# Sparse attention feeding a squared-ReLU feed-forward: batch 0's global columns in two groups of head pairs, batch 1's first pair loaded between weight slices, and batch 1's masks on VectorE

## The chip, the cores and the metric

The kernel runs on one core of a Trainium2 chip. A core has five engines [...]: TensorE (PE in the profile; its weight loads are PEld), VectorE (DVE), ScalarE (ACT), GpSimd (POOL) and SyncE (SP). SP, POOL and ACT can also start DMA transfers[...]. The metric is the device time of one execution in microseconds. Of seven runs before the change the median is 328.26 us, the lowest 325.69 and the highest 331.1.

## The reference

Attention over 8 batches, 8 heads, 576 tokens and 64 numbers per head, with a window of 32 tokens to each side and 8 global tokens that see all and are seen by all; its output is the input of a feed-forward with a squared ReLU.

```
scores = (1/sqrt(D)) * q @ k.T                       # B=8, H=8, S=576, D=64
mask   = |i - j| <= 32  or  i global  or  j global   # 8 global tokens, given as indices
attn   = softmax(where(mask, scores, -1e9))
x      = (attn @ v), heads side by side: (4608, 512)
out    = relu(x @ w_in)**2 @ w_out                   # w_in (512, 2048), w_out (2048, 512)
```

## The kernel before, in words

Heads are worked on in pairs, four pairs to a batch; the text calls them pairs 0 to 31, so pairs 0 to 3 are batch 0 and pairs 4 to 7 batch 1. `NHP` is 4. A pair's scores are computed in two halves of query columns (`half` 0 and 1): `sc_mm` is the matmul, `sc_exp` the exponential on ACT, `sc_mask` a multiplication by a 0/1 mask on DVE, `pv_mm` the product with the values, `pv_rec` a reciprocal on ACT by logarithm and exponential, and `pv_mul` the division that puts the result into the transposed activations `xT` (or `xA`, a second buffer, for the first half of batch 0). Where `added(i, half)` is true, the mask isn't multiplied on DVE: two matmuls of an identity with the tile `far` put a large negative number into the score bank ahead of the scores.

The queries of the global tokens are computed as extra columns of each half. `pv_sum` adds their partial sums and, at the last pair of a group, divides them (`gr`, `gx`); `scatter` then copies the 8 global columns, one at a time, into place on POOL. The columns of batch 0 go into `xA` and, once more, into `xT`.

The feed-forward's work is cut into units. The first chunk of 512 tokens uses `mm1_half` (256 tokens, two blocks of hidden units; 8 matmuls) and `mm2`; the rest uses `mm1` and a fast form of the second product. Units stand in the list `fills`; `take(n)` places n of them, and `fill(n)` places about n, as far as the batches that they read are done. They keep TensorE busy between the dependent steps of attention. A unit's result goes through ACT (`rl`, the ReLU) and DVE (`gt`, the square).

The whole order of work on each engine is written out by hand. For batches 0 and 1 tokens are loaded with their rows across partitions (`fetch_tokens`, on POOL's queue, which also casts to 16 bits), cast or copied by DVE (`cast_tokens`, tiles `natk` and `natq`), transposed on TensorE (`transpose`) and put in place by DVE and ACT (`place_k`, `place_q`). Batch 1's values are loaded as fp32 by 20 transfers on SP's queue (`fetch_values`, line 161; five per pair) into `stv`, and cast pair by pair by DVE (`cast_values`, line 463). Ahead of these transfers SP issues a tiny transfer called `gate` (line 1012), which reads the last slice of `w_in` and so holds SP until that slice has landed. From batch 2 on POOL first copies k and q into DRAM in another order (`kscr`, `qscr`; lines 178 and 185), SP adds the rows of the global tokens (lines 446 and 193), and SP then issues DMA transposes that bring `kt` and `qt` straight into SBUF (lines 201 and 202).

The part that the change touches lies at lines 971 to 1060. Its order on POOL before: the four slices of `w_in` (line 973), k and q of pairs 4 to 6, the scatter of batch 0's pairs 0 to 2 and then of pair 3 into `xA`, k and q of pair 7, the four slices of `w_out` (line 1009), the scatter into `xT` (line 1010), and the gathers and copies for batch 2. On TensorE: the first four units of `mm1_half` without their last quarter of the contraction, the value products of pairs 2 and 3 (half 1), the last quarter of the four units, two more units, the transposes of pair 4, two more units, and then the loop over pairs 4 to 7 (line 1032). After the loop come `scatter(1)`, the first DMA transposes and `fill(3)`; then the loop over pairs 8 to 31 (line 1063).

[...]

Of the kernel before, what the change touches and what calls it, by code (L numbers as in the profile page):

```python
# [50 lines left out]
def kernel(  # L51
# [18 lines left out]
    NDM = dm // P  # L70
    NFF = dff // P
    NHP = H // 2
# [9 lines left out]
    def sbt(name, shape, dtype, bufs=1, tag=None):  # L82
        return sb.tile(shape, dtype, name=name, tag=(tag or name), bufs=bufs)
# [12 lines left out]
    def pst(tag, shape, dtype=FP32):  # L96
        return psum["pool"].tile(shape, dtype, name=tag, tag=tag, bufs=psum["bufs"][tag])
# [12 lines left out]
    def token_rows(nm, i):  # L110
        x = "kq".index(nm)
        if i < 2:
            one = stf[0:TP, x, 2 * FW * i : 2 * FW * (i + 1)]
        elif i < NHP:
            one = s16a[0:TP, x, 2 * FW * (i - 2) : 2 * FW * (i - 1)]
        else:
            one = s16b[0:TP, x, 2 * FW * (i - NHP) : 2 * FW * (i - NHP + 1)]
        return one.rearrange("p (h f) -> p h f", h=2)
# [22 lines left out]
    xA = mix[:, 8 * FW : 8 * FW + NDM * S].rearrange("p (t s) -> p t s", t=NDM)  # L141
# [8 lines left out]
    def fetch_tokens(eng, nm, i):  # L150
        b, hp = divmod(i, NHP)
        eng.dma_start(
            out=token_rows(nm, i),
            in_=src[nm][b, 2 * hp : 2 * hp + 2].rearrange("h (p j) d -> p h (j d)", j=TJ),
        )
# [140 lines left out]
    def halves(to, weights, moving, **flags):  # L296
        for r in column_tiles():
            nc.tensor.matmul(to[r], weights[:, r], moving, **flags)  # L298
# [143 lines left out]
    def gather_store(c, gsts, nms="kqv", eng=None):  # L442
        for nm in nms:
            gst = gsts[nm]
            scr = dram.tile([P, D], gst.dtype, name=f"gscr_{nm}{c}")
            (eng or nc.sync).dma_start(out=scr, in_=gst)
            gscr[(nm, c)] = scr.rearrange("(b g h) d -> b g h d", b=2, h=H)
# [5 lines left out]
    def cast_tokens(op, nm, i):  # L453
        nat = nats[(nm, i)] = sbt("nat" + nm, [TP, TJ, P], FP16, bufs=2)
        op(
            out=nat.rearrange("p j (h d) -> p h j d", d=D),
            in_=token_rows(nm, i).rearrange("p h (j d) -> p h j d", d=D),
        )
# [100 lines left out]
    def mm1_half(u, half, tiles=range(NDM)):  # L559

        if 0 not in gts:
            gts[0] = sbt("gt", [P, NFF, TC], FP16)
        if 0 in tiles:
            ph_now[u] = pst("mm", [P, 2, 256])
        ph = ph_now[u]
        for j in range(2):
            for t in tiles:
                halves(
                    ph[:, j], w_in[:, t, (u + j) * P : (u + j + 1) * P],
                    (xT if half else xA)[:, t, half * 256 : half * 256 + 256],  # L570
                    start=(t == 0 and j == 0), stop=(t == NDM - 1), skip_group_check=True,
                )
        if NDM - 1 not in tiles:
            return
        rl = sbt("rl", [P, TC], FP16, bufs=5).rearrange("p (j x) -> p j x", j=2)
        nc.scalar.activation(out=rl, in_=ph, func=AF.Relu)
        nc.vector.tensor_tensor(
            out=gts[0][:, u : u + 2, half * 256 : half * 256 + 256], in0=rl, in1=rl, op=ALU.mult
        )
# [145 lines left out]
    def take(n):  # L725
        for _ in range(n):
            _, fn, a = fills.pop(0)
            fn(*a)
# [5 lines left out]
    def fill(n):  # L734
        credit[0] += n
        while fills and fills[0][0] <= done[0]:
            cost = {mm1: W1, mm2_fast: W2}.get(fills[0][1], 1) * share[0]
            if credit[0] < cost / 2:
                break
            credit[0] -= cost  # L740
            take(1)
        else:
            credit[0] = min(credit[0], 0)
# [6 lines left out]
    scs, ets, accs, recs = {}, {}, {}, {}  # L750

    def added(i, half):
        return i < NHP and (half == 0 or i < 2) or NHP <= i < 2 * NHP and half == 0

    def sc_mm(i, half, idles=0):

# [43 lines left out]
    def pv_mm(i, half, idles=0):  # L800
        b, hp = divmod(i, NHP)
        et = ets.pop((i, half))
        acc = pst("at", [P, 2, 512])
        warm(acc[:, 0], idles)
        win, _ = windows(i, half)
        vt = vts[i] if b < 2 else vbs[b % 2][:, :, 2 * hp : 2 * hp + 2]
        for n, (t, so, c0, w) in enumerate(win):
            o = c0 - half * BANKC
            for x in range(2):
                for e in range(2):  # L810
                    nc.tensor.matmul(  # L811
                        acc[D * e : D * e + D, x, o : o + w], onesb if x else vt[:, t, e],
                        et[:, e, so : so + w],
                        start=(n == 0), stop=(n == len(win) - 1), skip_group_check=True,
                    )
        accs[(i, half)] = acc[:, :, 0:BANKC].rearrange("p x (k c) -> p x k c", c=GRP)

    def pv_rec(i, half):
        av = accs[(i, half)]
        rec = recs[(i, half)] = sbt("rec", [P, 2, GTOK], FP32, bufs=3)  # L820
        nc.scalar.activation(out=rec, in_=av[:, 1, :, 0:GTOK], func=AF.Ln)  # L821
        nc.scalar.activation(out=rec, in_=rec, func=AF.Exp, scale=-1.0)  # L822

    def pv_sum(i, half):
        b, hp = divmod(i, NHP)
        av = accs[(i, half)]
        if half == 0 or b:
            if hp == 0 and half == 0:
                gsum[b] = sbt("gs", [P, 2, NHP, 2, NG], FP32, bufs=2)
            nc.vector.tensor_reduce(  # L830
                out=gsum[b][:, half, hp],
                in_=av[:, :, :, GTOK:GRP].rearrange("p e k g -> p e g k"),
                axis=AX.X, op=ALU.add,
            )
        if (half == 0 and b == 0 and hp >= NHP - 2) or (half and b and hp == NHP - 1):
            gs = gsum[b][:, 0]
            a, z = (0, NHP) if b else (0, NHP - 1) if hp < NHP - 1 else (NHP - 1, NHP)
            if b:
                nc.vector.tensor_tensor(out=gs, in0=gs, in1=gsum[b][:, 1], op=ALU.add)
            gr = sbt("gr", [P, NHP, NG], FP32, bufs=2)  # L840
            if a == 0:
                gxs[b] = sbt("gx", [P, NHP, NG], FP16, bufs=2)
            nc.vector.reciprocal(out=gr[:, a:z], in_=gs[:, a:z, 1])
            nc.vector.tensor_tensor(
                out=gxs[b][:, a:z], in0=gs[:, a:z, 0], in1=gr[:, a:z], op=ALU.mult
            )

    def pv_mul(i, half):
        b, hp = divmod(i, NHP)
        av, rec = accs.pop((i, half)), recs.pop((i, half))  # L850
        x0 = b * S + half * HS
        nc.vector.tensor_tensor(  # L852
            out=(xT if x0 else xA)[:, hp, x0 : x0 + HS].rearrange("p (k x) -> p k x", k=2),
            in0=av[:, 0, :, 0:GTOK], in1=rec, op=ALU.mult,
        )

    def pv(i, half):
        pv_mm(i, half)
        pv_rec(i, half)
        pv_sum(i, half)  # L860
        pv_mul(i, half)
# [8 lines left out]
    def scatter(b, pairs=slice(0, NHP), x=xT):  # L870
        xb = x[:, pairs, b * S : (b + 1) * S]
        for g in range(NG):
            nc.gpsimd.tensor_copy(out=xb[:, :, ds(gv[g], 1)], in_=gxs[b][:, pairs, g : g + 1])  # L873
# [5 lines left out]
    pool = nc.gpsimd  # L879
# [90 lines left out]
    sc_mm(3, 1)  # L970
    gather_store(0, gs0, "v")
    for i in range(4):
        pool.dma_start(out=w_in[:, :, ts(i, 512)], in_=wv[:, :, ts(i, 512)])
    def tokens1(i):
        for nm in "kq":
            cast_tokens(vec, nm, i)

    def transposes1(i):
        transpose("k", i)
        transpose("q", i)  # L980
        place_k(i, act)
        place_q(i)

    for i in range(NHP, 2 * NHP - 1):
        fetch_tokens(pool, "k", i)
        fetch_tokens(pool, "q", i)
    scatter(0, slice(0, NHP - 1), xA)
    pv_rec(1, 1)
    sc_exp(2, 1)
    sc_exp(3, 1)  # L990
# [3 lines left out]
    open_psum(2, 4)  # L994
    wide[0] = True
    for u in range(0, 8, 2):
        mm1_half(u, 0, range(NDM - 1))
    pv(2, 1)
    pv(3, 1)
    scatter(0, slice(NHP - 1, NHP), xA)  # L1000
    fetch_tokens(pool, "k", 2 * NHP - 1)
    fetch_tokens(pool, "q", 2 * NHP - 1)
    nc.scalar.copy(out=xT[:, :, 256:HS], in_=xA[:, :, 256:HS])
    for u in range(0, 8, 2):
        fills.pop(0)
        mm1_half(u, 0, range(NDM - 1, NDM))
    tokens1(NHP)
    for j in range(4):
        pool.dma_start(out=w_out[:, ts(j, 4), :], in_=wo[:, ts(j, 4), :])
    scatter(0)  # L1010
# [9 lines left out]
    nc.gpsimd.memset(vbs[0][96:P, NT - 1], 0.0)  # L1020
    gather_store(1, gs1)
    take(2)
    transposes1(NHP)
    tokens1(NHP + 1)
    take(2)
    done[0] = 1
    for vt in vts[NHP:]:
        nc.vector.memset(vt[96:P, 4], 0.0)
# [28 lines left out]
    scatter(1)  # L1057
    fetch_transposed(2 * NHP)
    fetch_transposed(2 * NHP + 1)
    fill(3)  # L1060
    wide[0] = False

    for i in range(2 * NHP, B * NHP):
        b, hp = divmod(i, NHP)
# [66 lines left out]
```

## Time and profile before

| what | value |
|---|---|
| median of 7 runs | 328.26 us (325.69 to 331.1) |
| the profiled execution, its own time | 327.39 us |
| its span, first to last instruction | 325.7 us |
| TensorE busy | 311.1 us, 96% of the span, 4739 matmuls |
| VectorE busy | 244.6 us, 75% |
| ScalarE busy | 202.0 us, 62% |
| GpSimd busy | 127.9 us, 39% |
| packets moved by POOL's queue, by SP's queue | 16.78 MB, 21.23 MB |
| granted TensorE clock | 1.000 |

The profile is one execution. Its own time exceeds the span by 1.69 us, which lies before the first and after the last instruction. A busy share is a mean over stages that differ much, so the stage from 15 to 71 us, in which the edits lie, has to be read by itself: by the order of the instructions on each engine, by what ended each wait, and by what the two DMA queues moved.

### The profile page before, as it was taken

How to read it: one execution, taken by the hardware profiler on the slowest of the kernel's cores; microseconds unless marked ns; L12 is line 12 of the kernel's file. 1: busy time of each engine (PE TensorE's matmuls, PEld its weight loads, DVE VectorE, ACT ScalarE, POOL GpSimd, SP SyncE). 2: the span in 40 equal slices, each digit the busy share in tenths (PEclk: the TensorE clock that was granted, in tenths of full speed). 3: DMA queues.
4: the chain of work that ended last, by engine and by line, in shares of the span. 5: the costliest groups of instructions: out<-in, count | busy, mean ns of one | idle time of the engine just before them, and what ended most of it. 6: DMA issues, size and time to landing. Idle time of an engine off the chain costs nothing.

```text
span 325.7 us, 11457 instructions
## 1 busy us (share of the span) xinstructions
PE 311.1 (96%) x4739; PEld 235.8 (72%) x4739; DVE 244.6 (75%) x601; ACT 202.0 (62%) x380; POOL 127.9 (39%) x222
## 2 busy tenths in 40 slices
PE   7996899989999999999999999999999999999995
PEld 4665677445578758875899856985698569868995
DVE  6576598548997788677867869876987698768465
ACT  3567687535866686667557387658765876373150
POOL 8466985548701960189100980049302000100000
PEclk9999999999999999999999999999999999999999
DMA  8999999999993999499924599769996301200211
GB/s 187 177 179 203 196 196 158 161 122 206 145 102 60 177 177 117 77 175 145 143 71 109 48 170 153 74 110 189 134 104 125 102 0 34 97 3 2 83 50 66
DMA packets 149919, 39.32 MB, mean 121 GB/s; under 512 B 133124, under 2 KB 149300, under 8 KB 149868
## 3 DMA queue, kind: packets, MB, share of 16 engines
q0 software_dynamic: 95408, 16.78, 68.2%
q1 hardware_dynamic: 54042, 21.23, 34.6%
q8 instruction: 37, 0.61, 0.8%
q10 hardware_dynamic: 418, 0.59, 0.7%
q14 instruction: 14, 0.11, 0.1%
HBM read 37.86 MB, written 17.29 MB: 169 GB/s over the span
## 4 chain that ended last, share of the span: by engine, by line
issue 36%; PE 29%; POOL 10%; DMA 8%; DVE 4%; ACT 2%; POOLq 1%; SPq 0%; ACTq 0%
PE mm L298 25%; DMA qscr<-in_q_dram 3%; POOL xT L873 3%; POOL kscr L178 3%; DMA kscr<-in_k_dram 2%; DMA qt<-qscr 2%; PE at L811 2%; POOL s16b L207 1%; PE at L770 1%; DVE gt L545 1%; ACT er L779 1%; DVE mix L630 1%; POOL qscr L185 1%; PE mm L492 1%; DVE early L624 1%
## 5 line engine op out<-in xcount | busy, mean ns | idle before, releaser
L298 PE MATMUL mm<-xT,w_in 128*64 128x512 f16 (+2 forms) x1216 | 122.5, 351 | 0.2 <-POOL xT L873 0.2
L298 PEld LDWEIGHTS <-w_in 128*64 128x64 f16 (+1 forms) x1280 | 79.3, 109 | 44.8 <-issue 3.3
L543 ACT ACTIVATE rl<-mm 128x512 f16<-128x512 f32 x128 | 75.0, 598 | 36.1 <-PE mm L298 34.0
L298 PEld LDWEIGHTS <-mix 128*64 128x64 f16 x1280 | 68.8, 110 | 1.9 <-issue 0.3
L545 DVE TENSOR_TENSOR gt<-rl 128x512 f16<-128x512 f16 x128 | 52.9, 422 | 22.9 <-ACT rl L543 22.0
L873 POOL COPY xT<-gx 128x4 f16 x64 | 18.0, 282 | 129.3 <-DVE xT L852 125.7
L779 ACT ACTIVATE er<-at 128x880 f16<-128x880 f32 x54 | 46.1, 904 | 15.5 <-PE at L770 13.9
L630 DVE TENSOR_TENSOR mix<-gt 128x1024 f16<-128x1024 f16 (+1 forms) x82 | 52.8, 670 | 0.2
L789 DVE TENSOR_TENSOR et<-er,mask 128x880 f16<-128x880 f16 x54 | 33.2, 616 | 17.8 <-ACT er L779 17.2
L298 PE MATMUL mm<-early,mix 128*64 128x256 f16 x768 | 45.4, 273 | 0.0
L821 ACT ACTIVATE rec<-at 128x288 f32<-128x288 f32 x64 | 25.8, 403 | 25.2 <-PE at L811 21.8
L298 PEld LDWEIGHTS <-gt 128*64 128x64 f16 (+1 forms) x596 | 33.1, 109 | 9.8 <-DVE gt L545 2.2
L852 DVE TENSOR_TENSOR xT<-at,rec 128x288 f16<-128x288 f32 x60 | 27.1, 452 | 8.1 <-ACT rec L822 7.7
L298 PE MATMUL mm<-early,gt 128*64 128x256 f16 x512 | 32.2, 274 | 1.0 <-DVE gt L545 1.0
L298 PE MATMUL mm<-w_out,mix 128*64 128x256 f16 x512 | 31.1, 273 | 0.0
L811 PE MATMUL at<-et,onesb 128*64 128x192 f16 (+5 forms) x400 | 29.8, 225 | 0.0
L822 ACT ACTIVATE rec<-rec 128x288 f32<-128x288 f32 x64 | 28.4, 443 | 2.0
L178 POOL DMA_DIRECT2D kscr<-in_k_dram x30 | 26.2, 1049 | 3.9 <-DMA w_out<-in_moe_w_out_dram 3.6
L665 DVE TENSOR_TENSOR ot<-mm,pt 128x512 f32<-128x512 f32 (+1 forms) x36 | 22.7, 630 | 6.7 <-ACT pt L690 5.4
L185 POOL DMA_DIRECT2D qscr<-in_q_dram x24 | 23.8, 1396 | 0.7 <-DMA gscr_k<-gstk 0.7
L770 PEld LDWEIGHTS <-kt 64*128 64x128 f16 x400 | 12.4, 96 | 15.0 <-issue 13.7
L690 ACT COPY pt<-mm 128x512 f32<-128x512 f32 (+1 forms) x18 | 9.7, 539 | 20.8 <-PE mm L298 20.8
(119 smaller groups left out, 340.0 us busy)
## 6 DMA issues: line engine op xcount, KB each, us to landing
out_dram<-ot SPq DMA_DIRECT2D x32, 256.0 KB
qscr<-in_q_dram POOLq DMA_DIRECT2D x24, 144.0 KB, 8.3
kscr<-in_k_dram POOLq DMA_DIRECT2D x24, 120.0 KB, 6.8
w_in<-in_moe_w_in_dram POOLq DMA_DIRECT2D x4, 512.0 KB, 8.9
w_out<-in_moe_w_out_dram POOLq DMA_DIRECT2D x4, 512.0 KB, 13.2
stf<-in_v_dram POOLq DMA_DIRECT2D x12, 120.0 KB, 10.3
s16b<-in_v_dram POOLq DMA_DIRECT2D x12, 120.0 KB, 8.5
early<-in_v_dram SPq DMA_DIRECT2D x20, 60.0 KB
```

Of the source, the lines that this page charges most:

```text
L178: nc.gpsimd.dma_start(out=kscr[b][r0 : r0 + KN[t]].rearrange("s (h d) -> s h d", d=D), in_=k[b, :, KT * t : KT * t + KN[t]].rearrange("h s ...
L185: nc.gpsimd.dma_start(out=qscr[b][r0 : r0 + GTOK].rearrange("s (h d) -> s h d", d=D), in_=q[b, :, GTOK * g : GTOK * (g + 1)].rearrange("h ...
L298: nc.tensor.matmul(to[r], weights[:, r], moving, **flags)
L543: nc.scalar.activation(out=rl, in_=ph, func=AF.Relu)
L545: nc.vector.tensor_tensor(out=gt[:, :, 0:T], in0=rl, in1=rl, op=ALU.mult)
L630: nc.vector.tensor_tensor(out=gsums[p][:, lo:hi, 0:TH], in0=g[0], in1=g[1], op=op)
L779: nc.scalar.activation(out=er[:, :, 0:W], in_=scs.pop((i, half))[:, :, 0:W], func=AF.Exp, bias=0.0, scale=scale)
L789: nc.vector.tensor_tensor(out=et[:, :, 0:W], in0=er[:, :, 0:W], in1=mask[:, MB[half] : MB[half] + W].unsqueeze(1).to_broadcast((P, 2, W)), ...
L811: nc.tensor.matmul(acc[D * e : D * e + D, x, o : o + w], onesb if x else vt[:, t, e], et[:, e, so : so + w], start=(n == 0), stop=(n == le ...
L822: nc.scalar.activation(out=rec, in_=rec, func=AF.Exp, scale=-1.0)
L852: nc.vector.tensor_tensor(out=(xT if x0 else xA)[:, hp, x0 : x0 + HS].rearrange("p (k x) -> p k x", k=2), in0=av[:, 0, :, 0:GTOK], in1=rec ...
L873: nc.gpsimd.tensor_copy(out=xb[:, :, ds(gv[g], 1)], in_=gxs[b][:, pairs, g : g + 1])
```

## The change

Seven edits. (1) `added` is no longer true for half 0 of pairs 4 to 7; those four scores are masked on DVE by `sc_mask`. (2) The global columns of batch 0 are divided and scattered into `xA` in the groups of pairs 0 to 1 and 2 to 3, not 0 to 2 and 3. (3) k and q of pair 4 are fetched between the second and the third slice of `w_in`. (4) On POOL the first scatter stands before k of pair 6, the second before q of pair 6, and k and q of pair 7 follow. (5) The first four `mm1_half` units are cut in the middle of the contraction, and the value products of pairs 2 and 3 (half 1) come after the transposes of pair 4. (6) The second `take(2)` ahead of the loop goes, so that these two units are placed in the loop. (7) `fill(3)` after the loop becomes `fill(5)`.

```diff
     def added(i, half):
-        return i < NHP and (half == 0 or i < 2) or NHP <= i < 2 * NHP and half == 0
+        return i < NHP and (half == 0 or i < 2)
...
-        if (half == 0 and b == 0 and hp >= NHP - 2) or (half and b and hp == NHP - 1):
+        if (half == 0 and b == 0 and hp % 2) or (half and b and hp == NHP - 1):
             gs = gsum[b][:, 0]
-            a, z = (0, NHP) if b else (0, NHP - 1) if hp < NHP - 1 else (NHP - 1, NHP)
+            a, z = (0, NHP) if b else (hp - 1, hp + 1)
...
     for i in range(4):
+        if i == 2:
+            fetch_tokens(pool, "k", NHP)
+            fetch_tokens(pool, "q", NHP)
         pool.dma_start(out=w_in[:, :, ts(i, 512)], in_=wv[:, :, ts(i, 512)])
...
-    for i in range(NHP, 2 * NHP - 1):
-        fetch_tokens(pool, "k", i)
-        fetch_tokens(pool, "q", i)
-    scatter(0, slice(0, NHP - 1), xA)
+    fetch_tokens(pool, "k", NHP + 1)
+    fetch_tokens(pool, "q", NHP + 1)
+    scatter(0, slice(0, 2), xA)
+    fetch_tokens(pool, "k", NHP + 2)
+    scatter(0, slice(2, NHP), xA)
...
     for u in range(0, 8, 2):
-        mm1_half(u, 0, range(NDM - 1))
-    pv(2, 1)
-    pv(3, 1)
-    scatter(0, slice(NHP - 1, NHP), xA)
+        mm1_half(u, 0, range(2))
+    fetch_tokens(pool, "q", NHP + 2)
     fetch_tokens(pool, "k", 2 * NHP - 1)
     fetch_tokens(pool, "q", 2 * NHP - 1)
     nc.scalar.copy(out=xT[:, :, 256:HS], in_=xA[:, :, 256:HS])
     for u in range(0, 8, 2):
         fills.pop(0)
-        mm1_half(u, 0, range(NDM - 1, NDM))
+        mm1_half(u, 0, range(2, NDM))
     tokens1(NHP)
+    transposes1(NHP)
+    pv(2, 1)
+    pv(3, 1)
...
     take(2)
-    transposes1(NHP)
     tokens1(NHP + 1)
-    take(2)
...
-    fill(3)
+    fill(5)
     wide[0] = False
```

## The prediction

> **What bounds the kernel now.** I read the page's busy shares first (TensorE 96%), then busy time by stretches around the edits, in the columns start:end, length, busy of PE, PEld, DVE, ACT, POOL, clock, DMA share, GB/s:
>
> ```profile
> 30.50:38.50 8.00, 6.55 (x72) 5.32 (x72) 3.50 (x9) 4.42 (x11) 7.20 (x16) 1.00 1.26 197
> ...
> 47.10:53.70 6.60, 6.60 (x96) 5.08 (x95) 5.60 (x17) 5.36 (x12) 3.01 (x5) 1.00 1.59 167
> 53.70:60.30 6.60, 6.60 (x81) 3.55 (x79) 5.95 (x18) 4.46 (x10) 5.88 (x7) 1.00 2.20 159
> 60.30:66.90 6.60, 6.40 (x68) 3.11 (x67) 2.62 (x8) 3.40 (x6) 1.20 (x2) 1.00 2.03 149
> 66.90:70.50 3.60, 2.74 (x14) 1.07 (x13) 1.33 (x5) 0.85 (x2) 1.21 (x7) 1.00 1.30 109
> ```
>
> In the loop over batch 1 (41.1 to 66.9) TensorE is full, but DVE is at 85 to 90% for pairs 5 and 6, and the DMA engines never rest. Next, the chain that ended last, from 62 us on (start, length, what):
>
> ```profile
> 62.59 1.03 SPq L201
> ...
> 63.83 6.55 DMA qt<-qscr
> 70.38 0.14 issue
> 70.52 0.56 PE at L770 x12
> ```
>
> Pair 8's scores start when its DMA transpose lands, at 70.5. TensorE, finished at 69.6, waited 0.87 us. After 71 us it loses little until 300, and the edits leave that order alone. So the time moves by what pair 8's scores move, and nothing can pull them far ahead of the transpose.
>
> The transfers before it, from SP's timeline and, below, the packets of the two queues (q0 POOL's, q1 SP's; packets, MB, share of the engines) from 32 to 36 us and from 36 to 49 us:
>
> ```profile
> 29.71 0.25 SPq L1012 DMA_DIRECT2D gate<-w_in  x1
> 30.28 0.29 SPq L1013 DMA_DIRECT2D early<-gscr_v  x1
> 30.61 9.50 SPq L161 DMA_DIRECT2D early<-in_v_dram  x13
> ```
>
> ```profile
> q0 software_dynamic: 570, 0.40, 66.8%
> q1 hardware_dynamic: 1291, 0.38, 60.1%
> ```
>
> ```profile
> q0 software_dynamic: 2147, 2.09, 96.8%
> q1 hardware_dynamic: 1783, 0.43, 24.6%
> ```
>
> Batch 1's values began while POOL, busy scattering, had let its own queue run low; in 4 us they moved as much as in the next 9. Beside `w_out` they get 1783 / 13 = 137 packets per us. A pair is 1,232 packets (576 rows x 2 heads, and 16 closing ones for each of five transfers), the globals 56. So pair 4's (1,232 + 56 of the 1,291) were there at 36.0, pair 5's at 36.0 + 1232/137 = 45.0. DVE casts them at:
>
> ```profile
> 42.88 0.56 DVE L463 CAST early<-early 128x512 f16<-128x512 f32 x2
> ...
> 47.94 0.55 DVE L463 CAST early<-early 128x512 f16<-128x512 f32 x2
> ```
>
> Cover: 6.9 and 2.9 us, less about 1 us of landing. DVE's list of waits has none on these loads.
>
> [...] 137 value packets beside 2147/13 = 165 weight packets per us. [...] SP sat 13.0 us at L1012 with all value loads behind it. [...] the 880-element masks take 0.616 us here, and I use that.
>
> **The change, part by part.**
>
> *Gate.* Two 96x768 loads now stand ahead of the third slice of `w_in`. They are 0.288 MB at about 200 GB/s: 1.45 us. The last slice lands at 29.7 + 1.45 = 31.2, and the 20 value loads on SP start 1.45 us later, first packets near 34.05 instead of 32.6.
>
> *POOL.* Before: q of pair 6 issued at 24.83, 16 scatter copies of 0.276 us from 27.27 to 31.68, k of pair 7 at 31.84. Now pairs 0 and 1 can be scattered once DVE has written them (25.07 + 0.43, plus 0.3 for a division that moves ahead): 8 copies, 25.85 to 28.05; k of pair 6; 8 copies to about 31.05; q of pair 6 at 31.2, then pair 7 and `w_out` from 33.1 to 36.1, as before. The same 16 copies, so no gain there. The 3.2 us that POOL waited for weight slices with k and q of pair 6 go [...], but only into the wait for DVE's columns. And POOL's queue now has one 144 KB load more to move after 33 us, just when the values come. Between 34 and 36.3 I give the values 240 packets per us (358 measured over 34 to 36 before, with POOL's queue still low at first), 540 in all, not 1,288. Then 137 per us: pair 4's values at 36.3 + 748/137 = 41.8, pair 5's at about 50.0 (`w_out` ends near 49.2; from there 2159 packets in 8 us, 270 per us, as before). With 1 to 1.5 us of landing, 43 and 51.2.
>
> *TensorE to the loop.* The start at 30.59 stays, behind the exponential that frees the score banks. 24 matmuls took 2.67 us, so 32 take 3.6: done at 34.2; the second group's columns (31.05) are there before the second half (32.4). The ReLUs no longer stand behind two value products: 4 x 0.49 to 35.0, squares to 35.4, `natk` 35.8; TensorE idles 34.2 to 35.85 (1.65 us; before, 1.12 + 0.29 near 36 and 38). Transposes 0.83, value products 0.9, two units 1.85: pair 4's scores at 39.4 instead of 41.1. But two units (1.85 us) are now owed, so this is worth nothing in itself: `take(2)` removed and `fill(5)` for `fill(3)` are the same work later.
>
> *Masks.* Four pairs of identity matmuls go: 4 x 0.37 = 1.48 us of TensorE. DVE gets 4 x 0.616 = 2.46 us and two squares of 0.42 more inside the loop. Pairs 5 and 6 had 5.60 and 5.95 of 6.60 busy, so DVE becomes as full as TensorE.
>
> *The late values.* [...] with `cast_values` of a pair stand, behind it, squares, masks, and the next pair's `kt` and `qt`. It wants pair 4's values at 41.65 (last squares 40.75, `natk`/`natq` 0.55, memsets 0.35) and gets them at 43: a stall of about 1.3, with TensorE's two owed units as cover (uncovered, 1.3 us). Then it runs as before plus a mask, wanting pair 5's values at 48.3 and getting them at 51.2. Behind: cast 0.55, two squares 0.75, mask 0.62; pair 5's first value product starts at 53.2, not 51.44.
>
> *Sum.* From there TensorE took 69.64 - 51.44 = 18.2 us to the end of its units. Add two units (1.8), subtract two identity pairs (0.74) and an idle 0.2, add 0.4 and 0.7 for the `qt` of pairs 6 and 7 that DVE, now saturated, places late: 20.15. Arrival 53.2 + 20.15 = 73.35, so pair 8's scores move from 70.52 to about 73.3: +2.8 us. On the profiled execution's 327.39 that is 330.2; the median of the runs lies 0.87 us above it, so about 331.1.
>
> *SP.* Value loads that end 3 us later also delay the stores behind them (52.30 before), their rows into `kscr` (57.89) and the transposes (62.38). I put the transposes at 64.4 and, at 6.4 to 7.9 us as before, landing at 72.3: just under TensorE's arrival. POOL's later scatter into `xT` (39.85 for 36.25, as pair 3's last product comes later) pushes `kscr`'s first copies to 48.2; `w_out` moves until 49.2 and the fourth and fifth copies wait for it as before, so about 0.5 us at most.
>
> *Unknowns.* The values' rate while k and q of pairs 6 and 7 flow: 137 as a lower end (pair 5's at 52.5: another +1.3), 358 as the upper (50.0 - 0.9: -1.2); I take 240. [...] the copies on POOL took 186 to 608 ns[...].
>
> **Rivals.** *A (forecast): late values starve DVE*, +1.3 to +4. For it: the packet rates and DVE's order. *B: values in time.* POOL's queue could run dry longer than I think (q of pair 6 issued 1 us later gives the values about 350 packets, 2.5 us). Then TensorE arrives at 69.64 - 1.48 - 1.6 (idle before) + 2.15 (idle now) = 68.7, but the transpose still lands at 70.4 to 71.5: -0.1 to +1.1, so 328.8. Against it: the later gate. *C, faster: the transposes run without company.* At 64 to 66 us they shared the engines with POOL's value copies (168% of the engines' time) and took 6.4 us; at 68 to 72 a `kt` took 4.0. If POOL's queue is empty when they start and the values are in time, they land 2.4 us sooner; that decides if SP issues them before 63.3 us. Then TensorE's 68.7 counts: -1.8 us, 326.5. Against it: SP's stores lie behind value loads that start later. *D: SP becomes the bound.* If the values end 4 us later, the transposes start at 66.5 and land at 73.5 to 74.5: +3.0 to +4.0, so 331.8. For it: the stores wait behind all 20 loads. *E: the scatter blocks TensorE.* If the POOL copies take 0.45 us each, the second group ends at 33.2 and TensorE waits 0.8 us; small, inside A.
>
> **How the numbers follow.** A 0.48, B 0.24, C 0.12, D 0.16. Half a per cent, 1.64 us, is about what a measurement of this kernel can tell from no change. A lies over it for 0.41 of its 0.48, else within (0.07); D over it for 0.15; B is within it but for 0.05 over and 0.02 below; C half of its runs below and the rest within, to which I add 0.05 for medians that scatter (seven runs span 5.4 us). Slower 0.61, same 0.26, faster 0.13. The time is A's, 331.0 (the sum rounded towards the other cases by 0.1). The range leaves out the better part of C and the far end of D, and takes in both ends of the unknown rate: 327.2 to 333.8. A alone: 329.5 to 332.5.
>
> **What would show it.** Gate near 31.2. A DVE wait on the value loads at L463, near 43 and longer near 51: the main step. Pair 4's scores near 39.4. DVE over 6.2 of 6.6 us in the loop. Transposes issued near 64.4, pair 8's scores near 73 with TensorE, not the transpose, arriving last or within 1 us of it. After that the same spacing. I am wrong if the values land by 48, or if the time moves after 75 us.

## The result, and the profile after

| what | before | after |
|---|---|---|
| median | 328.47 us (64 runs, 325.69 to 332.29 and two of 627) | 331.22 us (27 runs, 329.57 to 337.67) |
| ratio, 95% interval | | 1.009 [1.0072, 1.0108] |
| the profiled execution, its own time and span | 327.39, 325.7 us | 332.89, 331.2 us |
| its granted TensorE clock | 1.000 | 0.979 |
| TensorE busy, VectorE busy | 311.1, 244.6 us | 311.8, 246.6 us |

The changed kernel is 2.75 us slower by the medians. Ratios compare fast runs alone; left out are, among others, the two of before at 627 us and the one of after at 337.67 us. The two profiled executions differ by 5.5 us, twice as much: that of before lies 1.08 us below its median, that of after 1.67 us above. Sizes taken from this pair of profiles are therefore about twice too large, and the clock in the table says where to look for the difference.

Busy time by stretches, after the change, in the columns that the prediction gives (start:end, length, busy of PE, PEld, DVE, ACT, POOL, clock, DMA share, GB/s):

```profile
30.50:39.10 8.60, 6.61 (x64) 5.14 (x66) 3.55 (x9) 2.63 (x6) 5.66 (x10) 0.76 1.04 150
...
45.00:51.00 6.00, 5.46 (x86) 4.42 (x83) 4.69 (x13) 4.36 (x9) 5.35 (x7) 1.00 1.23 193
51.00:57.50 6.50, 3.55 (x34) 2.65 (x33) 4.90 (x14) 2.76 (x8) 5.63 (x7) 0.81 1.97 180
57.50:64.00 6.50, 6.50 (x89) 4.69 (x88) 5.87 (x17) 4.74 (x10) 4.54 (x6) 0.93 2.30 159
...
76.30:86.30 10.00, 10.00 (x118) 5.46 (x116) 8.34 (x16) 5.86 (x11) 9.09 (x11) 1.00 1.30 165
```

TensorE has a hole of 3 us between 51 and 57.5. From 76.3 on it is full again, with 118 matmuls in 10 us, as it was before from 71 on:

```profile
71.00:81.00 10.00, 10.00 (x119) 5.48 (x116) 8.39 (x16) 5.86 (x11) 9.06 (x11) 1.00 1.38 186
```

The time moved ahead of pair 8's scores, not after them.

SP's timeline, and the two queues from 34 to 36.3 us and from 36.3 to 49 us:

```profile
31.87 0.25 SPq L1017 DMA_DIRECT2D gate<-w_in  x1
...
32.77 21.37 SPq L161 DMA_DIRECT2D early<-in_v_dram  x20
54.26 0.39 SPq L446 DMA_DIRECT2D gscr_k<-gstk  x1
...
65.27 1.25 SPq L201 DMA_TRANSPOSE kt<-kscr  x1
```

```profile
q0 software_dynamic: 347, 0.24, 85.1%
q1 hardware_dynamic: 345, 0.15, 33.5%
```

```profile
q0 software_dynamic: 1974, 1.92, 93.5%
q1 hardware_dynamic: 1828, 0.44, 26.2%
```

The values get 345 packets in the first 2.3 us (150 per us) and 1828 in the next 12.7 (144 per us), where before they had 1,291 of their packets by 36 us. Pair 5's are the packets up to 2,520 (the globals' 56 and two pairs of 1,232). 2,173 are moved by 49 us, 153 in the next us and 312 in the one after, so the count is reached near 50.6. They land later: SP's value loads wait ten times for earlier ones, 6.3 us in all, and the 18th, which waits in the trace for the tenth, the last of pair 5, is issued at 52.73. Before, it was issued at 47.32, so that those rows had landed 1.0 us or more ahead of the cast that needs them (48.28). VectorE's waits from 36 to 75 us, which held no wait on these loads before, and its casts:

```profile
DVE early L463 <- DMA early<-in_v_dram: 3.0, 3, 2.0
```

```profile
43.71 0.43 DVE L463 CAST early<-early 128x512 f16<-128x512 f32 x1
44.92 0.23 DVE L463 CAST early<-early 104x128 f16<-104x128 f32 x1 [0.79 <-DMA early<-in_v_dram]
...
52.11 0.52 DVE L463 CAST early<-early 128x512 f16<-128x512 f32 x1 [2.05 <-DMA early<-in_v_dram]
52.81 0.23 DVE L463 CAST early<-early 104x128 f16<-104x128 f32 x1 [0.18 <-DMA early<-in_v_dram]
```

What TensorE made of it before, and what it makes of it now (start, length, what, and in brackets the idle time ahead with what ended it):

```profile
51.44 0.26 PE L811 MATMUL at<-et,early 128*64 128x160 f16 x2
```

```profile
30.87 5.45 PE L298 MATMUL mm<-mix,w_in 128*128 128x256 f16 x32 [1.36 <-ACT er L779]
37.94 0.43 PE L492 MATMUL mm<-identity,natk 96*128 96x96 f16 x6 [1.62 <-DVE natk L455]
...
41.58 0.36 PE L770 MATMUL at<-qt,kt 64*128 64x160 f16 x6
...
55.08 0.35 PE L811 MATMUL at<-et,early 128*64 128x160 f16 x2 [2.95 <-DVE xT L852]
...
55.96 3.13 PE L298 MATMUL mm<-xT,w_in 128*128 128x256 f16 x16
...
75.80 0.56 PE L770 MATMUL at<-qt,kt 64*128 64x160 f16 x12
```

The two squares behind the cast of 52.81 start at 52.95 (`gt`, L577), though ACT had their input ready at 49.90. Pair 5's first value product, which had no wait before, now waits 2.95 us behind VectorE, which had waited for the values. Pair 8's scores start at 75.80 instead of 70.52, with no idle time ahead: TensorE comes last, not the transpose. Two rows show what the prediction had nowhere: 32 matmuls take 5.45 us, and 16 take 3.13, where 16 of the same form took 1.92 elsewhere. TensorE ran slowly here. The clock column (0.76, 0.81, 0.93) agrees.

### The profile page after: what moved, and what is told of

The parts are those of the page before. It is cut to its first block, busy times and chain, and to the rows that moved or that the text cites. A ratio compares the mean times of both kernels' runs of the same rounds, so it can differ in the third digit from the quotient of the medians.

```text
span 331.2 us, 11444 instructions
## 1 busy us (share of the span) xinstructions
PE 311.8 (94%) x4731; PEld 236.0 (71%) x4731; DVE 246.6 (74%) x605; ACT 201.9 (61%) x380; POOL 125.9 (38%) x222
## 4 chain that ended last, share of the span: by engine, by line
issue 44%; POOL 23%; DMA 18%; PE 12%; POOLq 1%; SPq 1%; DVE 0%; ACT 0%
PE mm L298 12%; DMA kscr<-in_k_dram 6%; POOL kscr L178 5%; DMA w_out<-in_moe_w_out_dram 5%; POOL xT L873 4%; DMA early<-in_v_dram 4%; DMA qscr<-in_q_dram 3%; POOL qscr L185 3%; POOL s16b L207 3%; POOL stf L207 2%; POOL s16b L152 2%; POOL mix L873 1%; POOLq L873 1%; POOL w_in L976 1%; POOL gstk L435 1%
## 5 line engine op out<-in xcount | busy, mean ns | idle before, releaser
L298 PEld LDWEIGHTS <-w_in 128*64 128x64 f16 (+1 forms) x1280 | 80.7, 110 | 45.2 <-issue 2.1
L873 POOL COPY xT<-gx 128x4 f16 x64 | 17.2, 269 | 134.9 <-DVE xT L852 131.4
L779 ACT ACTIVATE er<-at 128x880 f16<-128x880 f32 x58 | 49.7, 904 | 16.8 <-PE at L770 15.2
L789 DVE TENSOR_TENSOR et<-er,mask 128x880 f16<-128x880 f16 x58 | 35.7, 616 | 19.0 <-ACT er L779 18.4
L811 PE MATMUL at<-et,onesb 128*64 128x192 f16 (+5 forms) x400 | 31.1, 230 | 0.0
L811 PEld LDWEIGHTS <-onesb 128*64 128x64 f16 x400 | 22.7, 113 | 0.7
```

The source lines that it names most:

```text
L779: nc.scalar.activation(out=er[:, :, 0:W], in_=scs.pop((i, half))[:, :, 0:W], func=AF.Exp, bias=0.0, scale=scale)
L789: nc.vector.tensor_tensor(out=et[:, :, 0:W], in0=er[:, :, 0:W], in1=mask[:, MB[half] : MB[half] + W].unsqueeze(1).to_broadcast((P, 2, W)), ...
L811: nc.tensor.matmul(acc[D * e : D * e + D, x, o : o + w], onesb if x else vt[:, t, e], et[:, e, so : so + w], start=(n == 0), stop=(n == le ...
```

## The experiments

Twelve runs in three groups, each with its own runs of the kernel before on the same chip; ratios are to those. All kernels compute the whole output. The expectations speak of theory A (pair 5's values come late, and VectorE, with squares and a mask behind their cast, holds TensorE up), of M (the masks fill VectorE, whenever the values come) and of P (TensorE's new order, with its gap ahead of the loop), and in the last group of the clock as a cause of its own. Numbers of the edits are those of the change.

| kernel | median, us | ratio to before | wait for values at L463, us (longest) |
|---|---|---|---|
| changed, again | 332.48 | 1.0102 [1.0052, 1.0153] | 3.9 (1.9) |
| changed, gate on an earlier slice | 328.31 | 0.9968 [0.9941, 0.9996] | none |
| changed, edit 3 undone | 330.89 | 1.006 [1.0032, 1.0087] | none |
| changed, edit 1 undone | 330.87 | 1.0045 [1.002, 1.0071] | 4.2 (2.7) |
| changed, edits 5 to 7 undone | 330.77 | 1.0058 [1.0032, 1.0084] | 2.3 (1.5) |
| before with edits 2 and 4 | 329.93 | 1.0039 [1.0012, 1.0065] | 1.2 (1.2) |
| before with edit 1 | 329.56 | 1.0035 [0.9998, 1.0071] | 3.1 (1.5) |
| before with edits 5 to 7 | 329.58 | 1.0033 [1.001, 1.0057] | 2.1 (1.8) |
| before with edit 3 | 328.77 | 1.003 [1.0002, 1.0057] | 2.6 (1.8) |
| before with the earlier gate | 329.26 | 1.0036 [1.0006, 1.0066] | none |
| changed, gap filled | 331.19 | 1.0096 [1.0065, 1.0126] | none |
| changed, gap filled, earlier gate | 327.24 | 0.9991 [0.9965, 1.0017] | none |

The waits come from one execution each, the ratios from many. The changed kernel itself ran in the second group, so that the other two compare with it across chips.

**The gate.** SP is let go by the second slice of `w_in` rather than by the last, and all else of the change stays.

```diff
-in_=w_in[0:1, 0, 3 * 512 : 3 * 512 + 8]
+in_=w_in[0:1, 0, 512 : 512 + 8]
```

> The changed kernel with one edit: the small gate transfer on SP's queue reads the second slice of w_in instead of the last, so that batch 1's value loads start some 6 us sooner. Theory A (late values starve VectorE): the wait of the casts at L463 on the value loads goes, pair 5's first value product starts near 52 instead of 55, pair 8's scores come near 71, and the time is 0.997 to 1.003 of the kernel before. Rival M (the masks fill VectorE): nothing of that depends on the loads, 1.006 to 1.010 stays. Rival P (TensorE's new order idles ahead of the transposes of pair 4): 1.006 to 1.010 stays too.

The loss is gone: 0.9968, against 1.009 for the change. The gate is issued at 23.96, no wait at L463 is left, and pair 5's first value product comes 2.3 us earlier. TensorE, then the windows of this kernel:

```profile
52.81 0.26 PE L811 MATMUL at<-et,early 128*64 128x160 f16 x2 [0.69 <-DVE xT L852]
...
72.94 0.56 PE L770 MATMUL at<-qt,kt 64*128 64x160 f16 x12
```

```profile
47.00:54.00 7.00, 6.31 (x95) 5.00 (x93) 6.63 (x19) 5.33 (x13) 6.96 (x9) 1.00 1.61 165
54.00:61.00 7.00, 6.07 (x91) 4.60 (x89) 6.63 (x19) 5.06 (x12) 7.00 (x8) 1.00 2.24 159
```

VectorE is busy 6.63 of 7.00 us twice, fuller than ever in the change itself, and by its ratio the kernel isn't slow. A full VectorE alone does not cost the 2.75 us. The late values do, or what comes with them: everything behind the gate on SP moves too, and the first transpose is issued at 59.92, not 65.27. This one execution took 330.78 us, against a median of 328.31. Pair 8's scores came at 72.94, not near 71 as expected, with no value late and no wait for the transpose; the mean granted clock was 0.66 from 30 to 41 us and 0.97 from 41 to 47, and 1.00 behind that. So a low clock goes with a loss of some 2 us here, without late values.

**The loads of pair 4 back behind the slices (edit 3 undone).**

```diff
-        if i == 2:
-            fetch_tokens(pool, "k", NHP)
-            fetch_tokens(pool, "q", NHP)
         pool.dma_start(out=w_in[:, :, ts(i, 512)], in_=wv[:, :, ts(i, 512)])
+    fetch_tokens(pool, "k", NHP)
+    fetch_tokens(pool, "q", NHP)
```

> The changed kernel with k and q of pair 4 fetched after all four weight slices again; all else as changed. Theory A: the gate falls back by about 1.5 us to near 30 us, pair 5's values land 1.0 to 1.5 us sooner but still after VectorE wants them, 1.003 to 1.006. Rivals M and P: the place of these two loads is nothing to them, 1.007 to 1.010.

1.006: the upper edge of A's range. The gate comes at 29.88, as expected. Against the expectation this profile has no wait at L463: the values' packets pass pair 5's 2,520 by 44 us (2,835 are moved), 5.4 us ahead of the cast (49.37). By the ratios 0.3% of the 0.9% hangs on these two loads, though the two intervals overlap, and 0.6% stays in a kernel whose one profile shows no late values. Either they are late in others of its executions, or something beside them costs; this run doesn't tell which.

**The masks back on TensorE (edit 1 undone).**

```diff
-        return i < NHP and (half == 0 or i < 2)
+        return i < NHP and (half == 0 or i < 2) or NHP <= i < 2 * NHP and half == 0
```

> The changed kernel with the masks of pairs 4 to 7 added on TensorE again (four pairs of identity matmuls, no four multiplications on VectorE). Theory A: pair 5's values are as late as before and TensorE has 1.5 us more to do, 1.007 to 1.012. Rival M: VectorE's 2.5 us are the cause, so with them gone 0.999 to 1.003. Rival P: 1.007 to 1.012.

Neither range holds 1.0045. The waits at L463 are as long as ever (4.2 us), and yet about 0.45% is won back. The prediction's sum has something for the masks, which the expectation left out: a mask behind the cast (0.62) and two `qt` that a full VectorE places late (0.4 and 0.7), less 0.74 for the identity matmuls, 1.0 us or 0.3% in all. The traces don't bear this out. In the change TensorE is idle for only 0.20 us between pair 5's first value product and pair 8's scores, so `qt` costs it nothing; and the one profile of this kernel, an execution of 333.45 us, has pair 8's scores at 75.82, as late as the change. By which way the masks cost, if they do, stays open, and the miss counts against A as the whole account.

**TensorE's order back (edits 5 to 7 undone).**

```diff
-        mm1_half(u, 0, range(2))
+        mm1_half(u, 0, range(NDM - 1))
+    pv(2, 1)
+    pv(3, 1)
...
-        mm1_half(u, 0, range(2, NDM))
+        mm1_half(u, 0, range(NDM - 1, NDM))
...
-    transposes1(NHP)
-    pv(2, 1)
-    pv(3, 1)
...
+    transposes1(NHP)
     tokens1(NHP + 1)
+    take(2)
...
-    fill(5)
+    fill(3)
```

> The changed kernel with TensorE's order of before: the cut of the first four units after three quarters, the value products of pairs 2 and 3 ahead of it, the transposes of pair 4 after two more units, both take(2), and fill(3). Masks, loads and scatters stay changed. Theory A: the values come as late, but TensorE owes no two units, 1.003 to 1.006. Rival P: 0.998 to 1.001. Rival M: 1.006 to 1.010.

1.0058, in A's range, well outside P's and just under M's (1.006): the new order isn't the sole cause, but by the ratio it isn't free either.

**The change again, and three parts alone.** The changed kernel unedited, and the kernel before with the named edits.

> The changed kernel itself, so that the single edits beside it are compared on the same chip. 1.007 to 1.011 of the kernel before, with a mean granted clock about 0.01 below its.

> The kernel before with the scatter edits alone (two groups of two pairs, the first ahead of k of pair 6, the second ahead of q of pair 6). Theory A (late values): POOL's queue is fuller when the values start, while the gate stays early; pair 5's values come about 3 us later than before, with 1 to 3 us of slack to cover it: 1.000 to 1.004. Rivals M and P: nothing of theirs is touched, 0.998 to 1.002.

> The kernel before with the masks of pairs 4 to 7 on VectorE alone. Theory A: the values are in time, VectorE becomes as full as TensorE, TensorE saves 1.5 us but the transposes for pair 8 stay: 0.998 to 1.002. Rival M: VectorE is over-full, 1.003 to 1.007.

> The kernel before with TensorE's order alone (edits 5, 6 and 7). Theory A: nothing is late, 0.998 to 1.003. Rival P: the idle stretch ahead of the transposes of pair 4 and the lower clock behind it cost 1.5 to 3 us, 1.004 to 1.009, with a mean granted clock at least 0.005 below that of the kernel before.

The change repeats: 1.0102, with a clock lower by 0.009, 3.9 us of waits at L463 and pair 8's scores at 75.94. Each part alone costs 0.3 to 0.4%, so that no single edit carries the loss. The scatter alone is in A's range (1.0039). For TensorE's order alone A expected at most 1.003 and got 1.0033; P, which expected at least 1.004 and a clock lower by 0.005, got a clock lower by 0.002. For the masks alone A expected at most 1.002 and got 1.0035; the interval reaches down to 0.9998, so the miss is small. But its profile shows why it was more than masks. The waits of VectorE, the queues from 32 to 36 us, and TensorE:

```profile
DVE early L463 <- DMA early<-in_v_dram: 3.1, 4, 1.5
```

```profile
q0 software_dynamic: 807, 0.58, 104.8%
q1 hardware_dynamic: 600, 0.22, 28.3%
```

```profile
52.97 0.26 PE L811 MATMUL at<-et,early 128*64 128x160 f16 x2 [2.69 <-DVE xT L852]
```

The values have 600 packets by 36 us here, not 1,291, and pair 5 waits for them almost as it does in the change. This execution ran at full clock throughout (1.000); its pair 8 came at 71.66, 1.1 us later than before, which is the wait without a lower clock and without the two units owed. Yet this edit touches nothing ahead of pair 4's scores: up to 39 us the work on POOL, SP and TensorE is that of the kernel before. What differs is the timing of this execution: POOL began the scatter at 25.78 instead of 27.27 and k of pair 7 at 30.57 instead of 31.84, while SP's gate came at 30.26 instead of 29.71. The head start of the values is thus not fixed by the program but differs by the execution. Even in the profile of before pair 5's values can be shown to have landed only 1.0 us ahead of their cast (by 47.32, for 48.28), so the kernel before may lose it too in some of its runs; it was profiled only once. For the same reason the waits at L463 in the other single-edit profiles can't be laid to their edits one by one.

**Earlier gate on the kernel before; edit 3 alone.**

> The kernel before with its gate transfer reading the second slice of w_in, the same edit as in the earlier run on the changed kernel. Theory A: pair 5's values had 1 to 3 us of slack there, so their earlier start frees nothing but SP's stores and the transposes for pair 8, which TensorE waits 0.9 us for: 0.994 to 1.000. If the early gate by itself is worth as much here as on the changed kernel (about 1.2%), 0.986 to 0.990, then late values are no cost of the change but one of both kernels, and theory A falls.

> The kernel before with k and q of pair 4 ahead of the third weight slice, alone. Theory A: the gate moves from near 29.7 to near 31.2, pair 5's values come 1.5 to 3 us later, against a slack of 1 to 3 us: 1.000 to 1.005, with a wait of VectorE on the value loads of up to 2 us. Rivals M and P: 0.998 to 1.002.

An earlier gate buys nothing without the change: 1.0036, over A's range, which ended at 1.000, and far from the 0.986 to 0.990 with which A would have fallen. It does what it should: no wait at L463, TensorE at its last unit's end at 68.6 instead of 69.6. But the transpose lands no sooner. TensorE's row there:

```profile
70.34 0.56 PE L770 MATMUL at<-qt,kt 64*128 64x160 f16 x12 [1.78 <-DMA qt<-qscr]
```

In that kernel POOL's copies into `kscr` wait 2.00 and 2.48 us for `w_out`, and the first transpose is issued at 62.36, where it was before (62.38). In the changed kernel with the earlier gate these copies run without such waits, since the scatter ahead of them comes later, and the transposes start 2.5 us sooner. So the earlier gate is no general gain that happens to hide the loss; it mends something that the change brings. Edit 3 alone gave 1.003, inside A's range.

All five kernels that differ from before in one thing lie between 1.003 and 1.0039, the earlier gate among them, from which a gain was expected. A third of a per cent may thus be what any disturbance of this hand-made order costs, or an offset of the comparison. Before was not run against itself, so this rival stands, and what single edits cost can't be read more finely than that.

**The gap ahead of `natk` filled.** The prediction sees TensorE idle for 1.65 us before pair 4's transposes. Here two units are placed in it; the second kernel has the earlier gate as well.

```diff
     tokens1(NHP)
+    take(2)
     transposes1(NHP)
...
-    take(2)
     tokens1(NHP + 1)
```

> The changed kernel with its take(2) moved ahead of the transposes of pair 4, so that two units fill the stretch in which TensorE idles for natk. Theory A alone: the values are as late, nothing gained, 1.008 to 1.011. With the clock as a second cause [...]: the mean granted clock rises by 0.004 or more and the time falls to 1.003 to 1.007.

> The changed kernel with both edits: the gate on the second slice, and take(2) ahead of the transposes of pair 4. Theory A: as with the gate alone, 0.995 to 0.999. With the clock as a second cause: a further 1 us and more, 0.990 to 0.995.

1.0096: filling the gap is worth nothing, as A alone had it, but the reason isn't A's. The mean clock of its runs is 0.984, as low as in the change (0.985), and in the profiled execution the 48 matmuls of the filled stretch take 169 ns each, as slow as the 32 of the change (5.45 us, 170 ns each), where 16 of this form took 1.91 us before (119 ns each):

```profile
33.56 8.10 PE L298 MATMUL mm<-mix,w_in 128*128 128x256 f16 x48 [1.36 <-ACT er L779]
```

This execution has no wait at L463: it starts these matmuls 2.7 us later than the change's did, so that VectorE comes to the casts after the values (pair 5's are cast from 52.04, without a wait), and pair 8's scores, at 75.56, wait 0.97 us for the transpose. A's ratio holds, then, but its wait isn't seen: here TensorE was late ahead of the casts, and whether late values would have cost the rest is hidden.

With the earlier gate it is 0.9991, a hair over A's range (0.995 to 0.999) and no better than the gate alone; the clock as a second cause expected 0.990 to 0.995. These two kernels are the one pair on the same chip that differs in nothing but the gate, and there the gate takes away the whole loss again, 1.05%. No version beats the kernel before by more than half a per cent; the change with the earlier gate (0.9968) is the nearest to it.

## Why the prediction was right

The time, 331.0, and the sign hold, and the loss hangs on the gate, as was forecast. An earlier gate, which brings the values forward and leaves all seven edits in place, took away the whole loss, twice. How much of it goes by way of VectorE's wait, the forecast's main step, is not shown. Step by step:

*Gate.* 31.87 for 31.2. Right, and 0.67 us late.

*POOL.* `w_out` starts at 33.27 for 33.1. The rate from 34 to 36.3 us was the wrong choice between two named ends: 150 packets per us, not 240, so 345 packets for 540. *Unknowns* gave 1.3 us for the lower end; as the values moved faster after 50 us, it came to 0.6 (the count of 2,520 near 50.6 for 50.0). The 358 per us of the profile before had pulled the choice up, and the masks-alone run shows that this figure itself was a chance of one execution.

*TensorE to the loop.* The idle time ahead of `natk` is right (1.62 for 1.65). The 32 matmuls are mis-sized: 5.45 us for 3.6, and so pair 4's scores come at 41.58, not 39.4. The granted clock, 1.000 in the one profile at hand, was taken as given. This costs little by itself, since pair 5's values land at 52.7 however early TensorE is.

*The late values.* The waits stand where they were put, at L463 near 44 and longer near 52. The casts that end them are at 44.92 and 52.81, for 43 and 51.2. For pair 5, 0.6 us of the 1.6 are the missing packets and most of the rest is the landing, for which 1 to 1.5 us were the author's estimate: by the next load's issue it took 2.1 us after the count of packets (52.73 after 50.6), and at most 2.3 before (47.32 after 45.0). So the cover of pair 5 before, which the prediction has at 2.9 less 1 us, can be shown for 1.0 us only. Behind the cast VectorE needs 2.27 us to the first value product, for 2.0.

*Sum.* Pair 5's first value product: 55.08 for 53.2. From there to pair 8's scores 20.72 us for 20.15, but with other parts. The late `qt` (0.4 and 0.7) cost nothing: TensorE is idle for 0.20 us in this stretch, as it was before, an idle time that the sum took off. In their place stands the clock. At half speed from 55.05 to 58.47, and busy for 3.39 us of it, TensorE lost an estimated 1.7 us, the half of that. The sum would then be 18.2 + 1.8 - 0.74 + 1.7 = 20.96, near the 20.72 measured. Together +5.28 us at pair 8's scores for +2.8, in an execution that was 1.67 us over its median, set against one that was 1.08 under.

*Masks.* "As full as TensorE" is wrong for the change itself (5.87 of 6.50 us): VectorE waits instead. It is right once the values are in time (6.63 of 7.00).

*SP.* Transposes at 65.27 for 64.4; stores 2.0 us later. Pair 8's scores don't wait for them, so D doesn't decide, nor E.

The agreement of 331.0 with 331.22 is better than its terms, and in part luck: 1.1 us forecast for `qt` never came, and the sum has no term for the clock, which did. In the runs that the ratios compare the changed kernel's mean clock is 0.985, and that of before 0.994 in the three later groups. Over these runs of before the time falls by 0.9 to 1.4 us for each 0.01 of clock (a fitted line in each group); with all runs taken in, by 1.3 to 2.0. So some 0.8 to 1.8 of the 2.75 us go with the lower clock. This is an estimate and not shown: no experiment held the clock and moved the rest. The two come together in part. A lower clock after 47 us appears in three of the ten profiles whose clock was read by stretches, the change, its repeat and the masks back (0.76 over 7 us in each), each time just after TensorE had waited 1.8 to 3.0 us behind late values. But it was lower ahead of any late value too: the mean from 30 to 41 us is 0.66 to 0.91 in the six of these profiles that are of changed kernels, and 0.90 to 1.00 in the four of before and of its single edits. What is left for waits and masks, about 1 to 2 us, is less than the 2.8 forecast.

Of the rivals, B and C describe the change with the earlier gate. It has the values in time, transposes issued at 59.92, ahead of the 63.3 that C asks for, and ends 1.05 us below before, between C's 326.5 and B's 328.8. Their premise failed in the change itself: the values were late. That transposes issued so early also land sooner, C's point, isn't seen: with the gap filled and the earlier gate they are issued from 60.98 on, and pair 8's scores still wait for them until 70.67, as B has it.

What stays open is how the 0.9% divides among the edits, and how much of it is the wait at L463 itself: the kernel with edit 3 undone and the one with the gap filled are slower than before by 0.6 and 1.0% with no such wait in the one execution that was profiled. Undone one by one they give back 0.3 to 0.5% each, alone they cost 0.3 to 0.4% each, the intervals are as wide as the differences between them, and a third of a per cent may be the price of any disturbance.

## What to carry to other kernels

When a change lets transfers of one queue start later, count the packets of the other queue that they now meet (beside `w_out` the values got 144 to 150 packets per us here, 358 per us from 34 to 36 in the profile before, with POOL's queue low at first), and follow the program's order on the receiving engine behind the first wait: what stands behind a late cast belongs to the price (here 2.27 us to the first value product). A head start read from one profile may be a chance of that execution; look for what makes it (here which of two queues gets going first), and take the end of the range that needs no luck. And judge a fix on both kernels: the earlier gate is worth 1.0 to 1.2% to the changed kernel and nothing to the old one, whose profile with it waits for the transpose.

## What the runs showed of the hardware

TensorE's granted clock falls within a kernel that keeps it busy 94% of the time. In the change's profile it is half (0.50) from 24.33 to 34.57 us and from 55.05 to 58.47, and full (1.00) between and after; the means of the stretches shown above (0.76, 0.81, 0.93) follow from that. The row of 32 matmuls from 30.87 on has 18 in its first 3.70 us, at 0.50, and 16 in the 1.75 us behind that, at 1.00 (those that lie across the border count twice). In the 3.42 us ahead of the first fall TensorE was busy for 1.08 us, in the 3.42 us ahead of the second for 0.50 us.

Not every stretch with so little work goes with a fall. In the masks-alone profile TensorE was idle for 2.69 us in one piece ahead of 52.97, and busy for 3.91 of the 6.60 us from 47.10 to 53.70; the clock is 1.00 there, and 1.000 over the execution. In the profile of before it was busy for 1.24 of the 3.42 us ahead of 30.59, at a clock of 1.00, and no fall follows. What decides it is not shown. The clock varies between executions of one kernel: the changed kernel's runs had mean clocks from 0.974 to 1.000, and one had 0.947.
